# A new DRAM layout for the streamed weights of a two-branch attention kernel: one block per DMA engine, blocks 648 KB apart

## The chip, the cores and the metric

The kernel runs on one core of a Trainium2 chip (trn2). The metric is device time of one execution in microseconds. Each figure is a median of several runs; profiled runs are within 0.5% of it.

## The reference, cut to what matters

```python
# x: 2048 tokens x 640; result g * A(x) + (1 - g) * B(x), g = sigmoid of a dot product
def _A_ref(x, wqkv, wo): ...          # sliding-window attention, 32 heads of 20, window 256
def _B_ref(x, mem0, Wq, Wk, Wv, Wo, seg_len):   # 64 segments of 32 tokens, one after the other
    for s in range(n_seg):
        h = jnp.concatenate([mem, xs], axis=1)            # 8 memory rows + 32 tokens
        q, k, v = (jnp.einsum('btd,dhe->bhte', h, W) for W in (Wq, Wk, Wv))   # 32 heads of 192
        ...                                               # masked softmax, p @ v
        o = jnp.einsum('bhte,hed->btd', o, Wo)
        mem = o[:, :M, :].copy()                          # the next segment needs it
```

Branch B is a recurrence: each of its 64 segments needs all of Wq, Wk, Wv and Wo, 7.9 MB each. The kernel keeps part of this in SBUF and reads the rest again in every segment.

## The kernel before

Weights are cut into units of 128 partitions: a q, k or v unit has 1536 bf16 columns (3072 bytes a partition), an o unit 1280 (2560 bytes). Of the units, 21 are streamed. While branch A runs, they are copied once into a packed DRAM buffer, where each unit is one contiguous piece of 384 KB. In branch B each segment loads them from there through a ring of four SBUF buffers, one copy issued from SP for each unit.

```python
class Weights:
    def __init__(self, nc, dram, Wq, Wk, Wv, Wo, streamed):
        ...
        self.slot = {u: n for n, u in enumerate(streamed)}
        self.packed = dram.tile([len(streamed), P, WQ], BF, name="w_packed")   # P = 128, WQ = 1536
    def dram_of(self, u):
        return self.packed[self.slot[u], :, 0:self.width(u)]
    def pack(self, u, engine):
        self.copy(u, self.dram_of(u), engine)
# ... in branch B
    sb = {"w": (4, [P, WQ]), ...}                       # ring of four
    def load_w(u):
        if u not in weights.slot:
            return None                                 # resident in SBUF
        b = sc.buf("w")
        sc.op("SP", 100 + 0.78 * weights.width(u),
              lambda: nc.sync.dma_start(tile_of(b)[:, 0:weights.width(u)], weights.dram_of(u)), writes=[b])
        return b
# ... one o-projection unit: 10 matmuls, 0.42 us of busy PE (270.6 us by 640)
            for r in range(2):
                for dt in range(KT):
                    nc.tensor.matmul(t[:, dt * L:(dt + 1) * L], lhsT=w[:, r * D + dt * P:r * D + (dt + 1) * P],
                                     rhs=OT["tile"][:, b, i, :], ...)
```

## Time and profile before

| | before |
|---|---|
| median time | 2614.36 us |
| recurrent branch, first to last streamed load | 699.0 to 2583.7 us |
| streamed loads | 1344 (21 in each of 64 segments) |
| SP's time to issue one | 320 ns |
| granted TensorE clock | 0.939 |

The prediction below shows the lines of the page that carry its argument. Two rows are added here. The first is from the page's busy times (engine, busy us, share, instructions), the second from its list of DMA issues (KB each, median us from issue to landing).

```profile
PE 2259.0 (86%) x49877; PEld 1665.6 (63%) x49893; DVE 1189.0 (45%) x3578; ACT 1115.8 (43%) x2433; POOL 602.1 (23%) x1782
...
t_w<-w_packed SPq DMA_DIRECT2D x704, 384.0 KB, 4.4
t_w<-w_packed SPq DMA_DIRECT2D x640, 320.0 KB, 4.3
```

The next rows, from the view of the streamed tile (us, times), are PE's matmul-side waits for streamed weights, which the prediction sums to 152 us:

```profile
  PE ps_o L762: 113.7, 178
...
  PE ps_q L597: 17.5, 24
  PE ps_v L597: 12.5, 23
  PE ps_k L597: 8.7, 19
```

### The profile page before, as it was taken

What the parts mean: (1) busy time and instruction counts of PE and PEld (TensorE: products, weight loads), DVE (VectorE), ACT (ScalarE), POOL (GpSimd) and SP (SyncE); (2) the same over time, 40 slices, a digit from 0 to 9 for tenths busy, and PEclk for the clock granted to TensorE, in tenths of its full rate; (3) what the DMA queues carried; (4) which work ended last, traced back from release to release, by engine and by line L of the source; (5) the groups of instructions that cost most, each with busy time, mean ns of one, the idle gap of its engine ahead of it and who ended that gap; (6) DMA issues with size and microseconds to landing.
All of it is one profiled execution on the core that took longest, in us unless ns stands there. A gap on an engine that the chain in (4) does not pass through costs nothing.

```text
span 2624.0 us, 113795 instructions
## 1 busy us (share of the span) xinstructions
PE 2259.0 (86%) x49877; PEld 1665.6 (63%) x49893; DVE 1189.0 (45%) x3578; ACT 1115.8 (43%) x2433; POOL 602.1 (23%) x1782
## 2 busy tenths in 40 slices
PE   7888888899788888888888888888888888888885
PEld 5777777699465666666655665666666665566663
DVE  5777777623243344434443343434443444334433
ACT  5777777722233333333333333333333333334333
POOL 7622222040122222222222222222222222122220
PEclk9999999999899999989999998999999999999997
DMA  6600000085588888888888888888888888888887
GB/s 215 196 17 17 20 17 15 21 262 150 158 277 264 284 276 264 288 275 281 266 276 271 284 268 266 274 282 275 270 285 272 275 282 273 264 269 283 279 274 236
DMA packets 299154, 591.76 MB, mean 226 GB/s; under 512 B 102552, under 2 KB 112032, under 8 KB 298656
## 3 DMA queue, kind: packets, MB, share of 16 engines
q1 hardware_dynamic: 275536, 525.43, 63.6%
q0 software_dynamic: 20160, 55.60, 6.5%
q8 instruction: 391, 6.41, 1.0%
q10 hardware_dynamic: 2960, 3.44, 0.4%
q14 instruction: 107, 0.88, 0.1%
HBM read 554.98 MB, written 36.97 MB: 226 GB/s over the span
## 4 chain that ended last, share of the span: by engine, by line
PE 51%; DMA 35%; ACT 10%; DVE 2%; issue 2%; SPq 0%; ACTq 0%; POOL 0%; DVEq 0%
DMA t_w<-w_packed 32%; PE ps_q L597 8%; PE ps_k L597 8%; PE ps_o L762 7%; PE ps_v L597 5%; ACT a_ex L195 4%; PE t_psum L438 4%; ACT a_pt L208 3%; PE qk_ps L124 3%; PE ps_pv L738 2%; PE tr_k L612 2%; PE t_psv L455 2%; PE S_ps L666 2%; PE pt_ps L205 1%; PE s_ps L187 1%
## 5 line engine op out<-in xcount | busy, mean ns | idle before, releaser
L597 PEld LDWEIGHTS <-t_hT 128*32 128x32 bf16 x15360 | 380.0, 99 | 310.2 <-issue 105.8
L762 PE MATMUL ps_o<-t_OT,t_w 128*128 128x40 bf16 x6400 | 270.6, 182 | 124.9 <-DMA t_w<-w_packed 113.7
L762 PE MATMUL ps_o<-t_OT,w_o 128*128 128x40 bf16 x8960 | 334.6, 182 | 42.0 <-ACT t_OT L743 41.7
L762 PEld LDWEIGHTS <-w_o 128*128 128x128 bf16 x8960 | 289.1, 98 | 49.5 <-issue 43.5
L762 PEld LDWEIGHTS <-t_w 128*128 128x128 bf16 x6400 | 210.6, 98 | 155.4 <-DMA t_w<-w_packed 152.1
L743 ACT CAST t_OT<-ps_pv 128x480 bf16<-128x480 f32 x256 | 143.2, 559 | 340.2 <-PE ps_pv L738 339.9
L195 ACT ACTIVATE a_ex<-s_ps,a_nmx 128x384 bf16<-128x384 f32 (+2 forms) x512 | 252.8, 576 | 64.2 <-DVE a_nmx L193 61.5
L644 POOL COPY t_K<-t_xqk 128x64 bf16<-128x64 bf16 x256 | 60.8, 237 | 947.8 <-PE S_ps L666 665.6
L193 DVE TENSOR_REDUCE a_nmx<-s_ps 128x1 f32<-128x384 f32 (+2 forms) x512 | 246.7, 523 | 32.4 <-PE s_ps L190 24.8
L602 ACT CAST t_tok<-ps_k 128x384 bf16<-128x384 f32 x256 | 122.7, 479 | 319.5 <-PE ps_k L597 319.5
L597 PE MATMUL ps_q<-w_q,t_hT 128*32 128x384 bf16 x4096 | 230.4, 348 | 18.7 <-DVE t_hT L773 18.4
L721 DVE TENSOR_TENSOR t_PTx<-PT_ps,mk_x 128x320 bf16<-128x320 f32 x256 | 125.2, 489 | 264.7 <-PE PT_ps L714 264.7
L597 PE MATMUL ps_v<-w_v,t_hT 128*32 128x384 bf16 x4352 | 230.1, 335 | 0.0
L597 PE MATMUL ps_k<-w_k,t_hT 128*32 128x384 bf16 x4096 | 226.3, 343 | 0.3
L635 DVE COPY t_K<-tr_k 128x256 bf16<-128x256 bf16 x256 | 74.0, 289 | 253.7 <-PE tr_k L612 252.4
L602 ACT CAST t_tok<-ps_q 128x384 bf16<-128x384 f32 x256 | 123.0, 481 | 137.7 <-PE ps_q L597 137.5
L187 PE MATMUL s_ps<-KT_blk,QTm 128*128 128x128 bf16 x1440 | 171.0, 223 | 6.0 <-ACT a_ex L195 5.6
L602 ACT CAST t_vtok<-ps_v 128x384 bf16<-128x384 f32 x256 | 122.7, 479 | 114.2 <-PE ps_v L597 112.9
L612 PEld LDWEIGHTS <-t_tok 128*128 128x128 bf16 x1536 | 87.7, 98 | 118.7 <-ACT t_tok L602 55.4
L773 DVE CAST t_hT<-ps_o 128x40 bf16<-128x40 f32 x63 | 12.6, 200 | 327.1 <-PE ps_o L762 327.1
L205 PE MATMUL pt_ps<-a_ident,a_ex 128*128 128x128 bf16 x1440 | 145.6, 220 | 8.5 <-ACT a_ex L195 1.2
L676 DVE TENSOR_REDUCE sm_mx<-S_ps 128x4 f32<-128x160 f32 x256 | 82.5, 322 | 149.0 <-PE S_ps L666 149.0
(138 smaller groups left out, 4606.2 us busy)
## 6 DMA issues: line engine op xcount, KB each, us to landing
t_w<-w_packed SPq DMA_DIRECT2D x704, 384.0 KB, 4.4
t_w<-w_packed SPq DMA_DIRECT2D x640, 320.0 KB, 4.3
xbqk<-t_qk SPq DMA_DIRECT2D x16, 768.0 KB, 5.1
t_xqk<-xbqk POOLq DMA_DIRECT2D x64, 192.0 KB, 4.7
w_v<-in_B_Wv_dram POOLq DMA_DIRECT2D x17, 384.0 KB, 7.1
w_q<-in_B_Wq_dram POOLq DMA_DIRECT2D x16, 384.0 KB, 5.2
w_k<-in_B_Wk_dram POOLq DMA_DIRECT2D x16, 384.0 KB, 6.5
xbv<-t_vt SPq DMA_DIRECT2D x64, 96.0 KB, 1.8
```

Source lines behind the costliest of these rows:

```text
L187: nc.tensor.matmul(sp[:, ci * P:(ci + 1) * P], lhsT=qm[r][:, g, :], rhs=kring[c][:, g, :], start=True, stop=not need_mask)
L193: nc.vector.tensor_reduce(out=nmx[:], in_=sp[:, 0:nk * P], axis=AX.X, op=ALU.max, negate=True)
L195: nc.scalar.activation(out=ex[:, 0:nk * P], in_=sp[:, 0:nk * P], func=ACT.Exp, bias=nmx[:], scale=1.0)
L205: nc.tensor.transpose(pt_ps[:, a, ci, :], ex[:, ci * P:(ci + 1) * P], ident[:])
L438: nc.tensor.matmul(pt[:, bb, :], lhsT=ws[ki][kt][:, c:c + P], rhs=xTb[:, kt, t * P:(t + 1) * P], start=(kt == 0), stop=(kt == KT - 1))
L597: nc.tensor.matmul(t[32 * j:32 * j + 32, 0:384], lhsT=tile_of(hT)[:, kt, :], rhs=w[:, j * 384:(j + 1) * 384], start=(kt == kts[0]), stop=( ...
L602: sc.op("ACT", act(384), lambda: nc.scalar.copy(tile_of(tok)[:], b["tile"][:, 0:384]), reads=[b], writes=[tok])
L612: nc.tensor.transpose(t[:, k, :], tok["tile"][:, k * P:(k + 1) * P], ident[:])
L676: nc.vector.tensor_reduce(out=x["mx"][:], in_=view(), axis=AX.X, op=ALU.max)
L721: nc.vector.tensor_tensor(out=tile_of(dst)[:], in0=PT["tile"][:, i, :, :].unsqueeze(2).to_broadcast([P, 2, 4, L]), in1=mk.unsqueeze(1).uns ...
L743: sc.op("ACT", act(480), lambda: nc.scalar.copy(tile_of(OT)[:].rearrange("p b j l -> p (b j l)"), o["tile"][:, 0:480]), reads=[o], writes= ...
L762: nc.tensor.matmul(t[:, dt * L:(dt + 1) * L], lhsT=w[:, r * D + dt * P:r * D + (dt + 1) * P], rhs=OT["tile"][:, b, i, :], start=(g == 0 an ...
```

## The change

The intent: each of the 16 DMA engines should read one contiguous run of a unit (8 rows, 24 KB), and the runs of different engines should lie far apart in DRAM. The packed buffer becomes 16 blocks of 27 slots of 8 rows, so that two blocks are 27 x 24 KB = 648 KB apart, and a load's source becomes 16 x 8 rows. The SBUF side remains 128 partitions in order.

```diff
-        self.packed = dram.tile([len(streamed), P, WQ], BF, name="w_packed")
+        assert len(streamed) <= 27
+        self.packed = dram.tile([16, 27, 8, WQ], BF, name="w_packed")
 ...
-    def copy(self, u, dst, engine):
+    def copy(self, u, dst, engine, packed=False):
 ...
-                engine.dma_start(dst[64 * a:64 * a + 64, r * D:(r + 1) * D], self.Wo[...])
+                part = slice(8 * a, 8 * a + 8) if packed else slice(64 * a, 64 * a + 64)
+                engine.dma_start(dst[part, ..., r * D:(r + 1) * D], self.Wo[...])
 ...
     def dram_of(self, u):
-        return self.packed[self.slot[u], :, 0:self.width(u)]
+        return self.packed[:, self.slot[u], :, 0:self.width(u)]
     def pack(self, u, engine):
-        self.copy(u, self.dram_of(u), engine)
+        self.copy(u, self.dram_of(u), engine, True)
```

More of the change, by code (lines that the diff above doesn't have):

```diff
@@ L391, in copy @@
             for a in range(2):
-                engine.dma_start(dst[64 * a:64 * a + 64, r * D:(r + 1) * D], self.Wo[8 * g + 2 * i + a, 64 * b:64 * b + 64, :])
+                part = slice(8 * a, 8 * a + 8) if packed else slice(64 * a, 64 * a + 64)
+                engine.dma_start(dst[part, ..., r * D:(r + 1) * D], self.Wo[8 * g + 2 * i + a, 64 * b:64 * b + 64, :])
     def load_resident(self, pool, u, engine):
@@ L564, in load_w @@
         b = sc.buf("w")
-        sc.op("SP", 100 + 0.78 * weights.width(u), lambda: nc.sync.dma_start(tile_of(b)[:, 0:weights.width(u)], weights.dram_of(u)),
+        sc.op("SP", 100 + 0.78 * weights.width(u), lambda: nc.sync.dma_start(
+            tile_of(b)[:, 0:weights.width(u)], weights.dram_of(u)),
               writes=[b])
```

## The prediction

> **What bounds the kernel now.** I read the views in this order: the 40 slices, the chain that ended last, busy time by stretch, the rows of the streamed weight tile, the waits of SP, and last the DMA packet records one by one. From the page:
>
> ```profile
> PE   7888888899788888888888888888888888888885
> DMA  6600000085588888888888888888888888888887
> GB/s 215 196 17 17 20 17 15 21 262 150 158 277 264 284 276 264 288 275 281 266 276 271 284 268 266 274 282 275 270 285 272 275 282 273 264 269 283 279 274 236
> ...
> PE 51%; DMA 35%; ACT 10%; DVE 2%; issue 2%; SPq 0%; ACTq 0%; POOL 0%; DVEq 0%
> DMA t_w<-w_packed 32%; PE ps_q L597 8%; PE ps_k L597 8%; PE ps_o L762 7%; PE ps_v L597 5%; ACT a_ex L195 4%; PE t_psum L438 4%; ACT a_pt L208 3%; PE qk_ps L124 3%; PE ps_pv L738 2%; PE tr_k L612 2%; PE t_psv L455 2%; PE S_ps L666 2%; PE pt_ps L205 1%; PE s_ps L187 1%
> ```
>
> The first quarter (branch A) has no DMA load; from slice 12 on (the recurrent branch) PE and the DMA engines both stand at eight tenths, and the landing of a streamed weight is the largest entry of the chain. The next view is busy time in stretches: PE, PEld, DVE, ACT, POOL, then granted clock, DMA share, GB/s.
>
> ```profile
> 1000.00:1500.00 500.00, 435.06 (x10805) 303.07 (x10806) 199.05 (x697) 183.74 (x426) 105.56 (x359) 0.95 0.87 276
> 1500.00:2000.00 500.00, 434.77 (x10711) 303.60 (x10709) 198.96 (x697) 182.80 (x425) 103.64 (x356) 0.93 0.86 273
> ```
>
> PE is 87% busy and DMA 87%: neither is saturated, they are coupled by a ring of four buffers. The view of the streamed tile says how tightly:
>
> ```profile
> L565 SPq DMA_DIRECT2D t_w<-w_packed x1344: 319/320/1599, 699.0 to 2583.7; - x192
> ...
> its engine sat idle before it (us, times) until:
>   DMA t_w<-w_packed: 304.5, 513
> ...
> DMA to landing us min/median/max: 2.7/4.3/7.5
> ```
>
> There are 1344 loads, 21 in each of 64 segments. They span 699.0 to 2583.7 us, so 1885 us: 29.4 us a segment, 1.40 us a load. Issuing one costs SP 0.32 us; landing takes 4.3 us. Four buffers over 4.3 us would allow one load every 1.07 us, were a buffer refilled at once; it isn't, since PE has to use it first. The 304.5 us counts the weight-load side of PE and the matmul side; the matmul side alone is 113.7 (o) + 17.5 (q) + 12.5 (v) + 8.7 (k) = **152 us**, in the rows "who waited for it". That, 5.8% of the span, is about all that faster loads can give back. SP's own waits complete the picture:
>
> ```profile
> SPq L565 <- PE ps_o L762: 327.6, 528, 2.4
> SPq L565 <- DMA t_w<-w_packed: 307.9, 446, 2.8
> SPq L565 <- PE ps_q L597: 186.0, 187, 1.7
> ```
>
> SP mostly waits for PE to free a buffer, so it is not short of issue time (1344 x 0.32 = 430 us of 1885); but what an issue takes comes after the buffer is freed, and so lies inside the lap of that buffer.
>
> Setting each landing in the trace beside the first PE instruction that uses it, 36% of the loads are used within 0.2 us of landing: PE was waiting for these. They gather in the o-projections, where PE needs a new unit every 0.4 to 0.7 us.
>
> **The packets.** A count over the packet records from 800 to 2500 us: packets of 3072 bytes (one partition row of a q, k or v unit) take 121 ns at the 10th percentile and the median, 154 ns on average, 733 ns at the 99th percentile. Those of 2560 bytes (an o unit) take 102 at the median, 125 on average. So the loads run at a floor of 25 bytes per ns and engine, with stalls in some tenth of the packets. The stalls sum to (154-121) x 84,208 + (125-102) x 76,096 packets, some 280 us of time per engine out of 1408. Following single engines, as far as the records allow, most of the stall falls on the first two or three of a load's eight rows. Their times have no sharp period of their own. This is what a change of the layout in DRAM can alter; it alters no byte count.
>
> [...]
>
> **The change, part by part.** (1) PE, DVE and ACT: the listing of the built program shows their order unchanged. Same matmuls, same 1344 loads, same bytes, same four buffers. (2) Packing: the same 51 copies of 384 or 80 KB on POOL, but spread over more of branch A (the scheduler expects them to cost more). They stay before the late resident loads, and POOL is 2 tenths busy there: 0 to 3 us either way. (3) Issue: the load becomes three-dimensional on both sides, and in the built program it loses a mark that all other copies of SP and ACT carry [...]. What the mark is worth no run shows yet. In this trace two-dimensional copies take SP 320 ns, marked three-dimensional stores 360, and POOL's copies 528 to 543. I choose 520 ns, as if the saving were gone: **+0.2 us a load**. (4) Stalls: unknown sign; I choose a small gain, because the engines read apart from each other, of **-0.1 us a load**.
>
> To turn time per load into span: a segment has 21 / 4 = 5.25 laps of the ring; with 36% of the loads on PE's path, a change d of the lap comes through as about 5.25 x 0.36 = 1.9 d a segment, or 64 x 1.9 = **121 d** over the run. Issue: 121 x 0.2 = +24 us. Stalls: 121 x -0.1 = -12 us. Sum +12 us, so 2614 + 12 = 2626.
>
> **The rivals.** Rival 1, the stalls are conflicts of engines that start neighbouring reads together, and 648 KB apart they vanish. The mean engine would gain (8 x 33 x 704 + 8 x 23 x 640) / 1344 = 0.23 us a load; a load lands with its slowest engine, and from first to last engine 1.5 us pass at the median, so up to 0.7 us. That makes 121 x -0.7 = -85, with the issue -61: some 2550. For it: the stalls sit at the start of loads. Against it: 24 KB and 648 KB are both 8 KB times an odd number, so any map of addresses that repeats at a power of two spreads the 16 engines alike.
>
> Rival 2, [...] If rows overlap half the time, a packet takes 60 ns more: 8 x (154 + 60) = 1.71 us a load, 36 us for 21 loads plus some 2 us of other traffic, against 29.4 now. DMA would be the bound: 64 x 8.6 = +550 us, some 3160. Against it: the loads of t_xv, from POOL, already have a source of 16 x 8 rows and 128 partitions; their 3072-byte packets show 121 ns at the 75th percentile even so.
>
> Rival 3, nothing at DRAM depends on the layout, and only the dearer issue counts: 2614 + 24 to + 33 (were it 0.27 us), some 2640. This is my likeliest single case.
>
> **Range and chances.** Stalls unchanged or little changed, 50%: 2610 to 2650, within 2%. Stalls mostly gone, 20%: 2530 to 2570, faster. Half gone, 10%: around 2585, within 2% or just beyond. Worse, from conflicts or ports, 20%: 2670 up to 3160; a still dearer issue adds a little there. So faster 0.24, within 2% 0.50, slower 0.26. The middle is 2626; 8 in 10 should lie between 2535 and 2750.
>
> **What would show it.** Issue: the duration of SP's t_w rows, 320 ns before; 500 or more confirms (3), 360 refutes it. Stalls: the mean of 3072-byte packets against the unchanged median of 121; below 135 is rival 1, a median well over 121 is rival 2. Landing: 4.3 us at the median should become 4.4. PE's 152 us of waiting for t_w should become some 165. DMA share stays near 0.87 in the middle stretches, and PE busy near 433 of 500. Branch A should end within 3 us of before. The prediction fails if the packet floor itself moves, if SP becomes short of issue time (over 1.4 us a load), or if slow packets come to hit the few o-units on PE's path more than the others.

## The result, and the profile after

The changed kernel takes 2926.90 us at the median (2919.67 to 2928.49, four runs) against 2614.36: 1.1187 times the time, with a 95% interval of 1.1163 to 1.1210. A ratio here is the mean time of one kernel's fast runs over the mean of the other's fast runs of the same rounds, so it is not quite the ratio of the medians. The predicted range ended at 2750.

The page of the changed kernel: busy times, the slices of PE, clock, DMA and GB/s, the chain, and the list of issues.

```profile
PE 2392.1 (82%) x49877; PEld 1723.5 (59%) x49893; DVE 1193.1 (41%) x3578; ACT 1119.3 (38%) x2433; POOL 602.4 (21%) x1782
...
PE   7888888897777778888887878788888787788885
...
DMA  6211100756989999999999899999999999999998
GB/s 231 74 49 30 40 19 9 235 147 161 235 226 236 230 240 239 239 241 241 241 235 232 235 240 238 240 235 238 235 236 238 240 235 231 233 243 242 247 233 225
...
DMA t_w<-w_packed 47%; PE ps_v L601 7%; PE ps_q L601 6%; PE ps_o L766 4%; ACT a_ex L195 3%; PE ps_k L601 3%; PE t_psum L441 3%; ACT a_pt L208 3%; PE ps_pv L742 3%; PE qk_ps L124 2%; PE pt_ps L205 1%; PE s_ps L187 1%; PE t_psv L458 1%; PE out_ps L255 1%; DMA xbv<-t_vt 1%
...
t_w<-w_packed SPq DMA_DIRECT2D x704, 384.0 KB, 5.9
t_w<-w_packed SPq DMA_DIRECT2D x640, 320.0 KB, 5.2
```

A stretch of the recurrent branch (busy time of PE, PEld, DVE, ACT, POOL, then granted clock, DMA share, GB/s), to stand beside the one in the prediction:

```profile
1000.00:1500.00 500.00, 407.34 (x9377) 277.04 (x9378) 173.71 (x605) 160.38 (x371) 91.35 (x311) 0.90 0.93 239
```

The DMA engines are busier (0.87 became 0.93), yet they move less: some 275 GB/s became 238. So each byte now costs more engine time. The share is a mean over 16 engines, and 14 that are busy all the time would make 0.88, so it is not that some engines were left out. The landing of a streamed weight rose from 32% to 47% of the chain. The wide units suffer more than the narrow ones now: 4.4 to 5.9 us, against 4.3 to 5.2.

The view of the streamed tile in the changed kernel:

```profile
L568 SPq DMA_DIRECT2D t_w<-w_packed x1344: 514/515/1554, 700.3 to 2884.6; - x192
...
  DMA t_w<-w_packed: 566.9, 734
...
  PE ps_o L766: 209.0, 261
...
  PE ps_q L601: 52.9, 80
  PE ps_k L601: 51.8, 85
...
  PE ps_v L601: 11.7, 22
...
DMA to landing us min/median/max: 3.6/5.6/9.0
```

SP needs 515 ns for an issue where it needed 320. PE waits 209.0 + 52.9 + 51.8 + 11.7 = 325 us on the matmul side for streamed weights, where it waited 152: 173 us more. PE's busy time grew by 2392.1 - 2259.0 = 133 us for the same matmuls. Together these are 306 us, and the span grew by 2924.5 - 2624.0 = 300.5 us. The first streamed load stands at 700.3 us (699.0 before), so all of it arose in the recurrent branch.

The second part, 133 us of busier PE, comes with a lower granted clock, 0.896 for 0.939. In every kernel that kept PE less busy than the kernel before did, the clock was lower: the slowest, e10_twice_0, had PE busy for 374 us of the stretch from 1000 to 1500 us, and its clock was 0.855; before had 435 us and 0.939; the fastest correct one, e9_ring6, had 459 us and 0.959. The clock's ratio, 0.939 / 0.896 = 1.048, would lengthen the 2259.0 us of before by some 108 us, most of the 133; this is an estimate. I take the lower clock for a consequence of the waiting; that is not shown, since no run changes one without the other.

The packet records tell what a packet costs. In this count, over the records of SP's queue from 800 to 2500 us of each kernel, 79% of the 3072-byte packets of before take 121 ns, give or take 2. After the change 21% do, 57% take 170 to 230 ns, and the median is 191. At the same time the long stalls (over 200 ns above the floor) fell from 220 us to 113 us of time per engine in that stretch. So two things moved in opposite directions, and the one to which my sum had given no room was the larger.

### The profile page after: what moved, and what is told of

It reads as the page before. It is cut to its first block, busy times and chain, and to the rows that moved or that the text cites. A ratio compares the mean times of both kernels' runs of the same rounds, so it can differ in the third digit from the quotient of the medians.

```text
span 2924.5 us, 113793 instructions
## 1 busy us (share of the span) xinstructions
PE 2392.1 (82%) x49877; PEld 1723.5 (59%) x49893; DVE 1193.1 (41%) x3578; ACT 1119.3 (38%) x2433; POOL 602.4 (21%) x1782
## 4 chain that ended last, share of the span: by engine, by line
DMA 50%; PE 38%; ACT 7%; DVE 2%; issue 1%; SPq 0%; POOL 0%; ACTq 0%; DVEq 0%; POOLq 0%
DMA t_w<-w_packed 47%; PE ps_v L601 7%; PE ps_q L601 6%; PE ps_o L766 4%; ACT a_ex L195 3%; PE ps_k L601 3%; PE t_psum L441 3%; ACT a_pt L208 3%; PE ps_pv L742 3%; PE qk_ps L124 2%; PE pt_ps L205 1%; PE s_ps L187 1%; PE t_psv L458 1%; PE out_ps L255 1%; DMA xbv<-t_vt 1%
## 5 line engine op out<-in xcount | busy, mean ns | idle before, releaser
L601 PEld LDWEIGHTS <-t_hT 128*32 128x32 bf16 x15360 | 408.2, 103 | 453.0 <-issue 266.6
L766 PE MATMUL ps_o<-t_OT,t_w 128*128 128x40 bf16 x6400 | 278.9, 185 | 213.3 <-DMA t_w<-w_packed 209.0
L766 PEld LDWEIGHTS <-t_w 128*128 128x128 bf16 x6400 | 217.4, 100 | 245.8 <-DMA t_w<-w_packed 241.4
L601 PE MATMUL ps_v<-w_v,t_hT 128*32 128x384 bf16 x4352 | 260.9, 369 | 0.0
L601 PE MATMUL ps_k<-w_k,t_hT 128*32 128x384 bf16 x4096 | 244.6, 364 | 0.0
L742 PE MATMUL ps_pv<-t_PTx,t_xv 128*64 128x160 bf16 x1536 | 155.8, 262 | 0.0
```

The costliest lines, as they stand in the source:

```text
L601: nc.tensor.matmul(t[32 * j:32 * j + 32, 0:384], lhsT=tile_of(hT)[:, kt, :], rhs=w[:, j * 384:(j + 1) * 384], start=(kt == kts[0]), stop=( ...
L742: nc.tensor.matmul(t[64 * a:64 * a + 64, 160 * b:160 * b + 160], lhsT=v[:, c:c + 64], rhs=p["tile"][:, a, :, :].rearrange("p j l -> p (j l ...
```

## The experiments

Three theories, guesses when they were made. **Destination** (rival 2 of the prediction; the expectations below call it the port theory): packets in flight together slow each other, depending on which SBUF partitions they are written to. My assumption was that a source of 16 x 8 rows and copies into partitions 0–63 or 64–127 bring the slow packets, and that copies into 32–95 do not. **Distance**: 648 KB between the engines' reads is bad for the DRAM. **Issue**: the 0.2 us more of SP's time a load, on every lap of the ring, is most of the loss.

All kernels below are edits of the kernel before, unless it is said otherwise. The table sums them up; the packet columns are of 3072-byte packets in SP's queue, 800 to 2500 us, the floor being 119 to 123 ns.

| run | what it changes | ratio to before (95%) | issue ns | median ns | mean ns | at the floor |
|---|---|---|---|---|---|---|
| before | | 1 | 320 | 121 | 154 | 79% |
| changed | 16 x 8, 648 KB apart | 1.1187 (1.1163–1.1210) | 515 | 191 | 190 | 21% |
| e8_changed | the same again | 1.1210 (1.1123–1.1296) | 515 | 189 | 189 | 22% |
| e1_unmarked | the mark of the issue alone | 1.0135 (1.0110–1.0160) | 451 | 121 | 157 | 81% |
| e2_shape_only | 16 x 8, 27 KB apart | 1.1071 (1.1044–1.1098) | 515 | 182 | 189 | 22% |
| e3_rows_apart | rows 81 KB apart | 0.9998 (0.9968–1.0029) | 320 | 121 | 155 | 79% |
| e7_blocks_of_4 | 32 x 4, 15 KB apart | 1.0232 (1.0156–1.0307) | 513 | 121 | 156 | 81% |
| e4_halves | partitions 0–63, then 64–127 | 1.1438 (1.1402–1.1474) | 2 x 596 | 196 | 195 | 19% |
| e10_twice_0 | both halves to 0–63 | 1.2467 (1.2355–1.2579) | 2 x 542 | 239 | 236 | 3% |
| e11_twice_32 | both halves to 32–95 | 1.0463 (1.0366–1.0561) | 2 x 588 | 121 | 152 | 80% |
| e9_ring5 | five ring buffers | 0.9611 (0.9554–0.9669) | 320 | 121 | 147 | 77% |
| e9_ring6 | six ring buffers | 0.9344 (0.9283–0.9405) | 320 | 121 | 144 | 69% |

### Issue alone: e1_unmarked

In the built program every copy from SP and ACT in the kernel before carries a mark (`dge_precook` in the edit), and the changed loads lack it. This run takes the mark from the streamed loads and leaves all else.

```diff
+        def f():                                        # (cut: f takes the place of the lambda)
+            nc.dge_precook = False
+            nc.sync.dma_start(tile_of(b)[:, 0:weights.width(u)], weights.dram_of(u))
+            nc.dge_precook = True
```

> The kernel before, same layout and same 128-row loads, only issued without the mark of the shorter issue path. Port theory ([...]): packets of 3072 B stay at 121 ns median, SP's issue rises from 320 to about 515 ns, time 2614 + 121 x 0.195 = about 2640 us. Issue theory (the dearer issue is what slowed the kernel): issue 515 ns and most of the 312 us, about 2850 us or more. If the mark is also what chooses the split over engines: packets near 191 ns and about 2920 us.

Measured: 2664.97 us against 2628.76 of before on the same chip. The tile's view of this run:

```profile
L568 SPq DMA_DIRECT2D t_w<-w_packed x1344: 450/451/1662, 697.4 to 2620.0; - x192
...
DMA to landing us min/median/max: 3.0/4.5/7.4
```

The mark is worth 0.13 us an issue (451 against 320), and that costs 1.35%, some 35 us. The expected 515 ns missed: the other 64 ns of the changed kernel's issue come with its shape, not with the mark. Packets keep their 121 ns, so the mark alone is not what slows them. The issue theory explains a part of the loss, and a small one. My own factor, 121 us of span per us of lap, would have given 16 us; it was half of what it should be.

### The shape without the distance: e2_shape_only

The changed kernel with all blocks of a unit together, one spare row after each eight so that the 16 x 8 shape remains.

```diff
-        self.packed = dram.tile([16, 27, 8, WQ], BF, name="w_packed")
+        self.packed = dram.tile([len(streamed), 16, 9, WQ], BF, name="w_packed")
-        return self.packed[:, self.slot[u], :, 0:self.width(u)]
+        return self.packed[self.slot[u], :, 0:8, 0:self.width(u)]
```

> The changed kernel's 16x8 loads, but the engines' blocks only 27 KB apart in DRAM, each unit in one place. Port theory: as the changed kernel, median packet about 190 ns, 2880 to 2950 us. Distance theory (blocks 648 KB apart collide in DRAM): packets back to 121 ns median, about 2640 us with the dearer issue left.

Measured: 2911.46 us, ratio 1.1071, median packet 182 ns. The view of the tile, and a stretch of busy times (PE, PEld, DVE, ACT, POOL, then clock, DMA share, GB/s):

```profile
L567 SPq DMA_DIRECT2D t_w<-w_packed x1344: 514/515/1758, 703.8 to 2872.9; - x192
...
DMA to landing us min/median/max: 3.5/5.6/8.0
```

```profile
1000.00:1500.00 500.00, 405.24 (x9336) 276.59 (x9328) 172.58 (x603) 158.70 (x368) 90.25 (x308) 0.89 0.93 239
```

Landing (5.6 us), DMA share (0.93) and 239 GB/s are those of the changed kernel. The shape brings the loss without the distance.

### The distance without the shape: e3_rows_apart

```diff
-        self.packed = dram.tile([len(streamed), P, WQ], BF, name="w_packed")
+        self.packed = dram.tile([P, 27, WQ], BF, name="w_packed")
-        return self.packed[self.slot[u], :, 0:self.width(u)]
+        return self.packed[:, self.slot[u], 0:self.width(u)]
```

> The kernel before with plain 128-row loads, marked, but each row of a unit 81 KB from the next in DRAM, [...]. Port theory: median packet 121 ns, about 2614 us; if distance eases the stalls of over 200 ns (halved in the changed kernel), 2540 to 2600. Distance theory: median packet towards 190 ns, 2800 us or more.

Measured: 2626.16 us, ratio 0.9998; issue and packets as before.

```profile
L565 SPq DMA_DIRECT2D t_w<-w_packed x1344: 319/320/1822, 702.5 to 2582.5; - x192
...
DMA to landing us min/median/max: 2.9/4.3/6.5
```

Here every row is 81 KB from the next, and nothing changes, for better or worse. The distance theory falls as the cause of the slow packets. So does the hope behind the change: the long stalls are 218 us per engine in this run and 220 before, so distance does not ease them. That they were halved in the changed kernel goes with its slower traffic, and e10_twice_0 below, the slowest, has the fewest (32 us); why is not shown.

### Two halves of 64 partitions: e4_halves

Another test of the destination: each copy writes 64 partitions, with the DRAM layout of before and plain two-dimensional copies.

```diff
+        def f():                                        # (cut: f takes the place of the lambda)
+            for p in (0, 64):
+                nc.sync.dma_start(tile_of(b)[p:p + 64, 0:weights.width(u)], weights.dram_of(u)[p:p + 64])
```

> The kernel before, each load cut in two of 64 partitions (0-63, then 64-127), same DRAM rows, issued without the mark (two issues of about 0.5 us). Port theory: [...] many packets near 190 to 240 ns, 2850 to 3050 us. Distance theory: packets at 121 ns, 2650 to 2700 us from the second issue.

Measured: 3006.52 us, median packet 196 ns (121 before). The slow packets appear with the old layout as well. But the issues doubled too, and in the built program the halves lack the mark (so do the copies of e10 and e11), so this run alone does not separate destination and issue; the pair e10 and e11 does.

### Blocks of four rows: e7_blocks_of_4

```diff
+        self.packed = dram.tile([len(streamed), 32, 5, WQ], BF, name="w_packed")
+        return self.packed[self.slot[u], :, 0:4, 0:self.width(u)]
 ...                                                     # (cut: the packing copies follow the new shape)
```

> The loads' source as 32 blocks of four rows, 15 KB apart, in place of 16 of eight. If the split over engines goes by plain sixteenths of the partitions whenever the two sides' slowest dimensions differ: median packet about 185 ns and about 2900 us, as with 16 blocks. If blocks of four [...]: packets at 121 ns and about 2660 us.

Measured: 2683.52 us, ratio 1.0232 (1.0156 to 1.0307), median packet 121 ns.

```profile
L566 SPq DMA_DIRECT2D t_w<-w_packed x1344: 512/513/1957, 703.8 to 2636.7; - x192
...
DMA to landing us min/median/max: 3.1/4.5/7.0
```

The first of the two expectations failed and the second held. With 32 blocks of four rows the two sides' dimensions still differ and the issue still costs 513 ns, yet packets run at their floor, 121 ns. So it isn't every mismatch that slows the packets; blocks of eight do (a median of 191 ns in the changed kernel) and blocks of four do not. Why is not shown. The run also sizes the issue at the changed kernel's price: some 2.3 of the 11.9 points (interval 1.6 to 3.1). If the two parts add, the other 9 to 10 are the slow packets.

### One half-size load, two destinations: e5_dst0 and e6_dst32

Both bring only the first 64 DRAM rows of a unit; they differ in the destination. Their result is wrong. The comparison with the reference passed even so, in these two and in e10 and e11: its tolerance does not see the streamed weights, and it is no proof of a layout.

```diff
-            nc.sync.dma_start(tile_of(b)[:, 0:weights.width(u)], weights.dram_of(u))
+            nc.sync.dma_start(tile_of(b)[0:64, 0:weights.width(u)], weights.dram_of(u)[0:64])     # e5_dst0
+            nc.sync.dma_start(tile_of(b)[32:96, 0:weights.width(u)], weights.dram_of(u)[0:64])    # e6_dst32
```

> Wrong result on purpose. The kernel before, but each load brings only its first 64 DRAM rows, into partitions 0-63 of the ring tile (the rest stays zero). [...] Port theory: a large part of the 3072 B packets at 170 to 240 ns, median well over 121. If ports play no part: as the next run, packet for packet.

> Wrong result on purpose. As the run before, the same 64 DRAM rows, the same shape and issue, but into partitions 32-95, [...]. Port theory: median packet 121 ns and under 10% of packets between 170 and 230 ns. If the slow packets come from the DRAM side or from the unmarked issue: the same packets as in the run before.

The two views of the tile, e5_dst0 first:

```profile
L565 SPq DMA_DIRECT2D b_w<-w_packed x1344: 444/445/1873, 705.2 to 2419.4; - x192
...
DMA to landing us min/median/max: 2.6/3.3/5.2
```

```profile
L565 SPq DMA_DIRECT2D b_w<-w_packed x1344: 488/489/2035, 705.1 to 2391.3; - x192
...
DMA to landing us min/median/max: 2.4/3.0/5.0
```

The expectation for e5_dst0 missed, and that for e6_dst32 held. The median packet of e5_dst0 is 121 ns too; 63% are at the floor, against 72% for e6_dst32, and 9% against 5% lie between 170 and 230 ns, so the direction alone is as forecast. But the landing is 0.3 us later with the same bytes, although its issue is even shorter; from the end of the issue to the landing it is 2.85 us against 2.36 at the median of the 3072-byte units. Why the median packet stayed at 121 ns is not shown. On the streamed packets the pair is inconclusive; the traffic was lighter than before (DMA share 0.57 and 0.55 from 1000 to 1500 us, for 0.87), and the next pair has more of it (1.02 and 0.84).

The loads of t_xv and t_xqk, in POOL's queue, tell more. No run edits them. Their 3072-byte packets, counted from 800 to 2300 us, take 185 ns at the median in e5_dst0 and 121 in e6_dst32. They take 121 ns in before, e1_unmarked, e3_rows_apart, e7_blocks_of_4, e11_twice_32 and with longer rings as well, but 196 in the changed kernel, 194 in e2_shape_only, 208 in e4_halves and 239 in e10_twice_0. A transfer that nobody changed slows down in just the runs for which the destination theory expects slow packets. The cause is then something that both transfers use, and not the DRAM layout of the slow packets themselves.

### The same with sustained traffic: e10_twice_0 and e11_twice_32

Each load is two copies of 64 rows, all 128 rows in sum, into a ring tile of twice the width, so that nothing is overwritten in flight. Their outputs are wrong, which doesn't matter for the times. To make room, `dynamic_dma_scratch_size` is cut to 4096 in both.

```diff
+            for i in range(2):                          # (cut: the rest of f; each run has one of the two lines)
+                nc.sync.dma_start(tile_of(b)[0:64, i * WQ:i * WQ + n], weights.dram_of(u)[64 * i:64 * i + 64])   # e10_twice_0
+                nc.sync.dma_start(tile_of(b)[32:96, i * WQ:i * WQ + n], weights.dram_of(u)[64 * i:64 * i + 64])  # e11_twice_32
```

> Wrong result on purpose. Each load is two copies of 64 rows, as in the run of two halves, but both go to partitions 0-63, into a ring tile of twice the width, so that no two copies write the same bytes. Port theory: [...] the DMA engines kept busy, median 3072 B packet 190 to 240 ns, about 3000 us. If destination partitions play no part: as the next run.

> Wrong result on purpose. As the run before, the same DRAM rows, number of copies and issue, but both copies of a load go to partitions 32-95: [...] Port theory: median packet 121 ns, 2640 to 2750 us, well over 200 us faster than the run before. If not ports: the same time and packets as the run before.

Measured: 3247.78 us into partitions 0–63, 2725.81 us into 32–95. A stretch of busy times, then the landing of the tile's view, for e10_twice_0 and then for e11_twice_32:

```profile
1000.00:1500.00 500.00, 373.62 (x8132) 253.74 (x8121) 152.86 (x531) 139.40 (x321) 79.34 (x272) 0.84 1.02 207
```

```profile
DMA to landing us min/median/max: 3.0/6.8/9.6
```

```profile
1000.00:1500.00 500.00, 425.38 (x10408) 295.87 (x10408) 193.92 (x680) 177.70 (x413) 100.80 (x348) 0.93 0.84 264
```

```profile
DMA to landing us min/median/max: 2.4/3.8/5.8
```

DRAM rows, bytes, copies and program order are the same, and an issue is even dearer in the faster run (588 against 542 ns). The destination alone makes 522 us, more than expected: e10_twice_0 was put at about 3000 us. Into 0–63 the engines are busy all the time (1.02, the records overlap a little) and move 207 GB/s; the median packet, 239 ns, is twice the 121 of the other run. The destination theory stands: under this traffic the partitions that are written decide. What the packets share there is not shown.

### The changed kernel again: e8_changed

> The changed kernel again, unedited, to stand beside the runs of this study on one chip: 2900 to 2930 us, ratio 1.11 to 1.12; SP's issue 515 ns, median packet of 3072 B near 191 ns.

Measured: 2922.96 us, ratio 1.1210, packets and issue as in the first run. The result holds on a second chip.

### A longer ring: e9_ring5 and e9_ring6

e1 showed that 0.13 us on the lap of a buffer costs 35 us. Then a longer ring should gain. The room comes from a smaller DMA scratch (`dynamic_dma_scratch_size`), 12288 and 8192 in place of the default.

```diff
-        "w": (4, [P, WQ]), ...
+        "w": (6, [P, WQ]), ...
-    nc = _bacc.Bacc("TRN2", target_bir_lowering=False, num_devices=1)
+    nc = _bacc.Bacc("TRN2", target_bir_lowering=False, num_devices=1, dynamic_dma_scratch_size=8192)
```

> The kernel before with five buffers in the ring of streamed weights in place of four; 3 KB a partition come from a smaller scratch of DMA descriptors. If the lap of a buffer (issue, landing, use) sets the time of the recurrent branch, as the dearer issue of the first experiment suggests (35 us for 0.13 us a load): PE's 152 us of waiting for streamed weights shrinks to under 80, 2520 to 2570 us. If the DMA engines' throughput sets it: within 1% of before.

> The kernel before with six ring buffers. Lap theory: a further but smaller gain over five buffers (2518 us), 2470 to 2510 us, since the DMA engines then near their limit (0.90 busy with five). If five already hide all waits: within 0.5% of five.

Measured: 2518.02 us with five, 2432.63 us with six, against 2626.23 and 2606.95 of before on their chips: ratios 0.9611 and 0.9344. The tile's view with five, then with six:

```profile
  DMA t_w<-w_packed: 183.0, 315
...
DMA to landing us min/median/max: 2.8/4.7/7.4
```

```profile
  DMA t_w<-w_packed: 79.9, 137
...
DMA to landing us min/median/max: 2.9/5.0/8.9
```

PE's waiting for streamed weights (both of its sides together) falls from 304.5 to 183.0 and 79.9 us, while a load takes longer to land, not shorter. Both times are below the expected ranges, with five just so; with five the matmul side still waits 83 us, where under 80 was forecast. No run changes the scratch alone, so a part of it in the gain is not ruled out; that PE's waits fall speaks for the ring. This version beats both kernels. Its loads have the addresses and bytes of before; whether the smaller scratch is safe for other inputs was not tried beyond these runs.

## Why the prediction was wrong, point by point

- **What bounds the kernel.** Right: the ring of streamed weights. The longer rings confirm it.
- **Part 1, order of PE, DVE and ACT; part 2, packing.** Right: the recurrent branch began at 700.3 us for 699.0.
- **Part 3, the issue.** Right in size: 0.2 us forecast, 0.195 measured. The reason given, the lost mark, makes 0.13 of it (320 to 451 ns in e1_unmarked), so that the size fits so well is in part luck. Mis-sized was what a lap costs: "a change d of the lap comes through as about 5.25 x 0.36 = 1.9 d a segment", 121 us of span per us. e1_unmarked gives 35 us for 0.13 us, so some 270, and e7_blocks_of_4 some 60 us (interval 42 to 80) for 0.193. I had counted only loads that PE already waited for; a later load makes others late as well. By the prediction's own count, 36% of the loads were used within 0.2 us of landing before; in the changed kernel 51% are. The tile's view shows 734 waits where there were 513. This explains a part of the larger factor; the rest stays open.
- **Part 4, the stalls. This is the step that failed.** "I choose a small gain, because the engines read apart from each other, of -0.1 us a load". Reading apart changed nothing at all (e3_rows_apart). What the shape did instead was to raise the median packet from 121 to 191 ns, and the median landing from 4.3 to 5.6 us. The issue is inside that time; from its end to the landing it was 3.96 us and became 5.03, so the step forecast as -0.1 us measured some +1.1. The sign that the prediction had named for rival 2, a median well over 121 ns, is the one that came.
- **Rival 1.** Refuted by e3_rows_apart (ratio 0.9998). The argument that any map repeating at a power of two treats 24 and 648 KB alike was on the right side, but it shows nothing by itself.
- **Rival 2**, the destination. Its sign came, and e10_twice_0 and e11_twice_32 show that the destination decides (239 and 121 ns); I had given it a share of the last 20%. I dismissed it on the loads of t_xv, which have the 16 x 8 shape and yet show 121 ns at the 75th percentile. That evidence was weak: each of those loads is only 16 packets of 3072 bytes, and they ran among streamed loads at 121 ns. In the changed kernel the packets of that size in POOL's queue, t_xv's among them, take 196 ns with nothing changed in their own layout. Its time, 3160 us, was too high for two reasons. I added my 60 ns, half of a packet's 121, to all of the old stalls: 154 + 60 = 214 ns, where the mean became 190. And the sum took all 21 loads of a segment for wide units, although 10 are narrow; with 11 x 8 x 214 ns, 10 x 8 x (125 + 51) ns and the same 2 us, the same working gives 34.9 us a segment and some 2970 us, an estimate that would have been near. Measured are 34.1 us a segment (2184.3 us by 64) at a DMA share of 0.93, so the engines came near to being the bound and did not quite become it.
- **Rival 3.** The dearer issue alone, "some 2640", so +26 us, was about half of what the issue costs: some 60 us in e7_blocks_of_4 (2683.52 us).

What stays open: the records name neither engine nor partition, so how a load of 16 blocks of eight or of 32 blocks of four is divided over the engines, and why the first has slow packets, is not shown. That it is the destination in the changed kernel too is inferred from e2, e7, e10 and e11 and from the packets in POOL's queue. Between e2_shape_only (1.1071) and the changed kernel (1.1187, 1.1210) lies about one point that no run on one chip has tested; it may belong to the distance. The long stalls are 142 us per engine in e2_shape_only, for 113 and 117 in the two runs of the changed kernel; with the 16 x 8 shape the distance may still ease them.

## What to carry to other kernels

When a DMA's shape is changed, ask what it does to the writing side, and not only which DRAM addresses it will read: the same rows took 239 ns a packet into partitions 0–63 and 121 into 32–95, and a source of 16 blocks of eight rows cost 11.9% where 32 blocks of four cost 2.3%, all of the latter plausibly the dearer issue. Evidence from another transfer in the trace counts only if it runs under the traffic that the one in question will make. Where a ring of buffers is bound by its lap, try one more buffer first: here the fifth gained 3.9% and two gained 6.6%, where no layout tried gained anything.
